# First unit of a sparse attention and its feed-forward layer: k and q loaded in turns, scores of each head pair as soon as it is there, masks as biases

## Chip, core and metric

The kernel runs on one core of a Trainium2 chip. The metric is the device time of one execution in microseconds (us), the median of several runs. PE is the tensor engine, DVE the vector engine, ACT the scalar engine, POOL is GpSimd and SP the sync engine.

## The reference

A block-sparse attention (4 batches, 8 heads, 768 positions, head size 64) is followed by a feed-forward layer with a quick GELU (3,072 tokens, width 512, inner width 2,048):

```python
k_sum = k.reshape(B, H, nb, 32, D).max(axis=3)      # 24 blocks of 32 positions
v_sum = v.reshape(B, H, nb, 32, D).mean(axis=3)
scores_l = where(abs(i - j) < 16, scale * q @ k.T, -1e9)
scores_s = scale * q @ k_sum.T + log(32)
a = softmax(concat([scores_l, scores_s]))
x = a @ concat([v, v_sum])                           # (tokens, 512)
h = x @ w_in
out = (h * sigmoid(1.702 * h)) @ w_out
```

Each query sees its neighbours within 15 positions and all 24 block rows. Inputs and output are float32 in HBM.

## The kernel before

The work is cut into eight *units* of 384 tokens, two for each batch. A unit has an attention part (scores, exponentials, values, normalization, transposition to `xT`) and a feed-forward part: `ff_in` makes 16 tiles `nt` of 128 inner columns (`ph`, then the GELU on ACT into `gT`), `ff_out` multiplies by `w_out` in 12 steps, called *slots*, of four matmuls (`po`). PE executes its instructions in the order in which the program writes them. The attention of a unit is laid between the feed-forward steps of the unit before it. The first unit has nothing to lie between: its attention is written out by hand, line by line, ahead of the loop over units. It covers batch 0, positions 0 to 383, and treats heads in four *pairs* `p`.

Every engine keeps the order of the program text (`keep_in_program_order`), so a line's place decides what stands behind it on its engine. An instruction that waits holds up all that follow on that engine.

The names for the first unit:

- `load_k(p)` loads one pair's keys in float32 as two DMAs, one from SP (first half of the positions) and one from ACT (second half); `load_q(p, 0)` loads the pair's first-half queries as one DMA, from SP for even and from ACT for odd pairs. The DMAs of these two queues share eight completion semaphores in turn, so that the ninth and later ones wait for an earlier landing before they are issued.
- `load_v0`, `load_w_in`, `load_w_out` and the second half of q (`load_q(p, 1)`) are issued from POOL. v and the weights are cast on the way.
- `cast_k`, `cast_q` make bfloat16 copies on the engine named; `k_turn`, `q_turn` transpose on PE; `k_own`, `q_copy` copy the result out of PSUM. `k_max` takes the block maxima.
- `s_turn(p)` makes the near scores of a pair in a PSUM tile of 1,024 columns (tag `big`, two buffers, shared with `k_turn`); `s_exp` is the exponential on ACT. `b_turn`, `b_exp` do the same for the block rows, `v_sum`, `v_copy` for the block sums of v; `av_near`, `av_blocks`, `v_norm` make the values; `x_turn` transposes them for the feed-forward part.
- Masks: `masks0` builds a tile on POOL by `affine_select`. Pairs 0 and 1 are multiplied by a tile of ones and zeros after the exponential (`s_mask`, on DVE); pairs 2 and 3 get a bias of -30000 from a matmul of that tile with the identity, ahead of the scores.
- `busy(n)` is n matmuls on zeros that nobody reads; `warmth(8)` the same, larger.

After the first unit, `plan0` says at which slot of the first unit's `ff_out` the second unit's attention is done: `q0` to `q3` transpose and copy the queries of the second half (`q_turn(i, 1)` and `q_copy(i, dve, 1)`, in the `big` buffers), `s0` to `s3` are scores, `v0`, `v1` values. The casts of these queries, `cast_q(dve, p, 1)`, stand after `ff_in` of `nt` 12 (pairs 0, 1) and 13 (pairs 2, 3). Slot -1 comes after the last `ff_in`:

```python
    plan0 = {-1: ["q0", "q1"], 0: ["q2", "q3"], 1: ["s0", "s1"], ...
```

For the third unit (batch 1), POOL loads k, v and q of that batch after w_out, and later writes the block-sum rows of v (`sum_dmas`, tile `vw` from `vs`).

Of the kernel before, what the change touches and what calls it, by code (L numbers as in the profile page):

```python
# [10 lines left out]
BF16 = mybir.dt.bfloat16  # L11
# [24 lines left out]
def kernel(  # L36
# [16 lines left out]
    NP = H // 2  # L53
# [51 lines left out]
    def load_v0(h0, h1):  # L105
        if h0 == 0:
            early["v"] = stage.tile([128, H, NJ, VC], BF16, name="vb", tag="vf")
            dve.memset(early["v"][..., D:VC], 1.0)
        pool.dma_start(out=early["v"][:, h0:h1, :, 0:D].rearrange("p h j d -> p (h j) d"),
                       in_=v[0, h0:h1].rearrange("h s d -> (h s) d")  # L110
                       .rearrange("(a p) d -> p a d", p=128))
# [68 lines left out]
    pool.affine_select(out=bm, in_=bm, compare_op=ALU.is_ge, fill=0.0, base=nb - 1,  # L180
                       pattern=[[block, 4]], channel_multiplier=-1)
    mk = consts.tile([128, NQ, QT], BF16, name="mk")
    mks = outp.tile([128, 2, 512], BF16, name="mk0", tag="osb")
    mk0, mk1 = mks[:, 0], mks[:, 1]
    dve.memset(mk0, 0.0)
    dve.memset(mk1, 1.0)
    BEFORE, AFTER, SIDE = HALF, HALF + 2 * window, 2 * window

    def masks0(mk0, fill):

        def out(ap, base, pattern, cp):
            pool.affine_select(out=ap, in_=ap, compare_op=ALU.is_ge, fill=fill,
                               base=base, pattern=pattern, channel_multiplier=cp)

        own = mk0[:, 0:HALF].rearrange("p (j c) -> p j c", c=128)
        out(own, window - 1, [[0, JH], [1, 128]], -1)
        out(own, window - 1, [[0, JH], [-1, 128]], 1)
        out(mk0[:, BEFORE:AFTER].rearrange("p (j c) -> p j c", c=window),
            -(128 - window + 1), [[0, JH - 1], [-1, window]], 1)
        out(mk0[:, AFTER:512].rearrange("p (j c) -> p j c", c=SIDE),  # L200
            -(SIDE - window + 1), [[0, JH], [1, SIDE]], -1)
# [83 lines left out]
    def cast_k(eng, p, half=None):  # L285
        if ("k", p) in cast:
            t = cast["k", p]
        else:
            if p == 0:
                kb2[0] = castp2.tile([128, NP, 2, JH, 2, D], BF16, name="kb", tag="kb")  # L290
            t = kb2[0][:, p]
        if half is None:
            copy(eng, t.rearrange("p e r h d -> p h (e r) d"),
                 raw["k", p].rearrange("p h e r d -> p h (e r) d"))
        else:
            copy(eng, t[:, half].rearrange("p r h d -> p h r d"), raw["k", p][:, half])
        cast["k", p] = t
# [38 lines left out]
    def busy(n):  # L336
        ps = pmm.tile([128, 512], F32, name="ps_w", tag="mm")
        for i in range(n):
            pe.matmul(out=ps[:, 0:128], lhsT=warm[:, 0:128], rhs=warm[:, 0:128],
                      start=True, stop=True)  # L340
# [66 lines left out]
    def k_turn(p):  # L407
        src = cast.pop(("k", p))
        big = st["K", p] = psb.tile([128, 1024], F32, name="ps_k", tag="big")
        for half in range(2):  # L410
            for r in range(JH):
                pe.matmul(out=at(big, half * 512 + r, [[JH, 128]]),
                          lhsT=src[:, half, r].rearrange("p h d -> p (h d)"),
                          rhs=ident, start=True, stop=True)
# [4 lines left out]
    def k_own(p, eng):  # L419

        copy(eng, own_keys(p).rearrange("p (e c) -> p e c", e=2),
             at(st["K", p], 0, [[512, 2], [1, HALF]]))

    def k_max(p):
        dve.tensor_reduce(out=ks0[p], in_=own_keys(p).rearrange("p (n c) -> p n c", c=block),
                          axis=AX.X, op=ALU.max)
# [25 lines left out]
    def s_turn(p):  # L452

        big = st["S", p] = psb.tile([128, 1024], F32, name="ps_s", tag="big")
        bias = p >= NP - 2
        if bias:
            for h in range(2):
                pe.matmul(out=big[:, h * 512:(h + 1) * 512], lhsT=ident, rhs=mk0, start=True,
                          stop=False, skip_group_check=True)

        def part(col, kj, q0, n):
            for h in range(2):
                r = slice(h * 64, h * 64 + 64)
                pe.matmul(out=big[:, h * 512 + col:h * 512 + col + n],
                          lhsT=own_keys(p)[r, kj * 128:(kj + 1) * 128],
                          rhs=qT[p][0][r, q0:q0 + n], start=not bias, stop=True,
                          skip_group_check=True)

        for j in range(JH):
            part(j * 128, j, j * 128, 128)  # L470
            part(AFTER + j * SIDE, j + 1, j * 128 + 128 - SIDE, SIDE)
            if j:
                part(BEFORE + (j - 1) * window, j - 1, j * 128, window)
# [9 lines left out]
    def s_exp(p):  # L483
        a = a_sb[p] = attp.tile([128, 2, 512], BF16, name="a_0", tag="a_sb")
        act.activation(out=a.rearrange("p h c -> p (h c)"), in_=st["S", p], func=ACT.Exp, scale=scale)

    def s_mask(p):
        dve.tensor_mul(a_sb[p], a_sb[p], mk1.unsqueeze(1).to_broadcast([128, 2, 512]))

    def b_turn(p):  # L490

# [113 lines left out]
    a_sb, x_sb, x2 = {}, {}, {}  # L605
# [330 lines left out]
    def exp_soon():  # L936
        act.activation(out=gate[:, 1:2], in_=gate[:, 0:1], func=ACT.Exp)


    dve.memset(gate, 0.0)  # L940
    for p in range(NP):
        load_k(p)
    exp_soon()
    for p in range(NP):
        load_q(p, 0)
    clear0(dve)
    dve.tensor_copy(out=identx, in_=ident)
    dve.memset(vs[:, :, D:VC], float(block))
    masks0(mk1, 0.0)
    warmth(8)  # L950

    cast_k(dve, 0, 0)
    cast_k(dve, 0, 1)
    k_turn(0)
    busy(3)
    cast_k(pool, 1, 0)
    cast_k("dve_alone", 1, 1)
    k_turn(1)
    busy(4)
    load_v0(0, 2)  # L960
    k_own(0, act)
    cast_k(act, 2, 0)
    cast_k(dve, 2, 1)
    load_v0(2, 4)
    load_v0(4, H)
    k_own(1, act)
    k_turn(2)
    busy(6)
    cast_k(dve, 3, 0)
    k_max(0)  # L970
    k_own(2, act)
    cast_k(act, 3, 1)
    cast_q(dve, 1, 0)
    cast_q(pool, 0, 0)
    k_turn(3)
    busy(4)
    cast_q(pool, 3, 0)
    k_own(3, act)
    q_turn(0)
    q_turn(1)  # L980
    k_max(1)
    cast_q(act, 2, 0)
    masks0(mk0, -30000.0)
    q_copy(0, dve)
    load_w_in(0, 512)
    busy(4)
    s_turn(0)
    q_copy(1, dve)
    q_turn(2)
    s_exp(0)  # L990
    q_turn(3)
    s_turn(1)
    k_max(2)
    q_copy(2, dve)
    load_w_in(512, 1024)
    b_turn(0)
    s_exp(1)
    q_copy(3, dve)
    b_turn(1)
    s_turn(2)  # L1000
    b_exp(0)
    v_sum(0)
    s_mask(0)
    s_turn(3)
    s_exp(2)
    load_w_in(1024, 1536)
    s_mask(1)
    v_copy(0)
    k_max(3)
    av_near(0)  # L1010
    s_exp(3)
    av_blocks(0, 0, D + 1)
# [43 lines left out]
    for p in range(NP):  # L1056
# [7 lines left out]
    plan1 = {0: ["t0"], 1: ["t1"], 2: ["s0", "s1"], 4: ["t2"], 5: ["t3"],  # L1064
             6: ["v0", "s2", "s3"], 8: ["x0"], 9: ["v1", "S0", "S1"], 11: ["x1", "S2", "S3"]}

    plan0 = {-1: ["q0", "q1"], 0: ["q2", "q3"], 1: ["s0", "s1"], 3: ["s2", "s3"], 6: ["v0", "v1"],
             9: ["x0"], 10: ["x1"]}

    w51 = vw[1].rearrange("p (j e) h c -> p j e h c", e=2)  # L1070
# [23 lines left out]
    for u in range(2):  # L1094
        todo = {}
        if u == 0:
            for p in range(NP):
                todo.setdefault(12 + p // 2, []).append(lambda p=p: cast_q(dve, p, 1))
        else:
            def value_rows():  # L1100
                vsum(1, range(NJ))
                block_sums()
                halo_dmas(w51, 0)
                sum_dmas(w51, 0)
                load_kc(2, range(6, H))
                load_vc(2)
                load_qc(2)

            todo = {0: [lambda: tk(0, 1)], 3: [lambda: tk(1, 1)], 5: [lambda: v_odd(1)],
                    9: [value_rows], 10: [lambda: tk(2, 1)], 13: [lambda: tk(3, 1)]}  # L1110
            ff_in(u, range(3))
        for nt in range(0 if u else N0, NT):
            if u == 0 or nt > 2:
                ff_in(u, (nt,))
            for f in todo.get(nt, ()):
                f()
        exp_soon()
        if u == 0:
            beside(1, -1)
            load_qc(1)  # L1120
            load_kc(2, range(6))
        order = [(ms, part) for ms in range(JH) for part in range(4)]
        if u == 0:

            order = [(ms, part) for part in range(4) for ms in range(JH)]
        for i, (ms, part) in enumerate(order):
            ff_out(u, ms, part)
            beside(u + 1, i)
            if u == 0 and i in (4, 7, 10):
                w_sums(i // 3 - 1)  # L1130
            if u == 1 and i == 2:
                w_sums(3)
            if u == 1 and i == 3:
                for g in range(2):
                    xk(g, 2)
# [122 lines left out]
```

## Time and profile before

| | us |
|---|---|
| median of four runs | 209.33 |
| lowest and highest | 208.01, 209.46 |
| profiled execution | 207.51 |
| its span, first to last instruction | 205.8 |
| PE busy | 198.3 |
| DVE busy | 146.9 |
| ACT busy | 124.6 |
| POOL busy | 92.7 |

The profile is of one execution; times in it are counted from the start of the span. Its rows name the engine, the operation and the tiles (out<-in). Nearly all instructions carry the line of the helper that keeps program order (L28), so one goes by the names of tiles: `kf`, `qf`, `vb` are the loaded k, q, v of batch 0; `kb`, `qb` their bfloat16 copies; `kx`, `qT` the transposed ones; `ps_...` PSUM tiles; `ph` and `po` the products of the feed-forward part. A busy PE is not PE at its peak, as ends of matmuls are modelled.

### The profile page before, as it was taken

What the parts mean: (1) busy time and instruction counts of PE and PEld (TensorE: products, weight loads), DVE (VectorE), ACT (ScalarE), POOL (GpSimd) and SP (SyncE); (2) the same over time, 40 slices, a digit from 0 to 9 for tenths busy, and PEclk for the clock granted to TensorE, in tenths of its full rate; (3) what the DMA queues carried; (4) which work ended last, traced back from release to release, by engine and by line L of the source; (5) the groups of instructions that cost most, each with busy time, mean ns of one, the idle gap of its engine ahead of it and who ended that gap; (6) DMA issues with size and microseconds to landing.
All of it is one profiled execution on the core that took longest, in us unless ns stands there. A gap on an engine that the chain in (4) does not pass through costs nothing.

```text
span 205.8 us, 5594 instructions
## 1 busy us (share of the span) xinstructions
PE 198.3 (96%) x2218; PEld 135.6 (66%) x2219; DVE 146.9 (71%) x423; ACT 124.6 (61%) x237; POOL 92.7 (45%) x165
## 2 busy tenths in 40 slices
PE   7799999999999999999999999999999999999993
PEld 2577655556655566566888866567888855568882
DVE  7698845798956769936757688589985856669331
ACT  2678677626675589677644657678627477881220
POOL 8968889399998953516998100301000000000000
PEclk9999999999999999999999999999999999999999
DMA  6999999999999999999999997993053250000323
GB/s 185 294 160 204 236 247 218 182 156 238 157 159 170 128 140 182 167 145 124 121 141 193 113 280 150 151 139 64 0 143 89 68 164 0 3 2 25 106 76 102
DMA packets 95010, 28.94 MB, mean 141 GB/s; under 512 B 82880, under 2 KB 92000, under 8 KB 94984
## 3 DMA queue, kind: packets, MB, share of 16 engines
q0 software_dynamic: 67920, 14.88, 84.2%
q1 hardware_dynamic: 25432, 12.53, 29.9%
q10 hardware_dynamic: 1632, 1.18, 1.9%
q8 instruction: 17, 0.28, 0.6%
q14 instruction: 9, 0.07, 0.1%
HBM read 27.26 MB, written 6.29 MB: 163 GB/s over the span
## 4 chain that ended last, share of the span: by engine, by line
PE 89%; DMA 4%; DVE 3%; ACT 1%; issue 0%; ACTq 0%; DVEq 0%
PE ph L28 31%; PE px L28 16%; PE po L28 10%; PE pw L28 8%; PE px_in L28 5%; PE ps_s L28 4%; PE py L28 4%; PE ps_av L28 4%; PE pw_in L28 4%; DMA kf<-in_k_dram 2%; DMA qf<-in_q_dram 2%; PE ps_t L28 1%; DVE qT L28 1%; PE ps_x L28 1%; PE ps_vs L28 1%; ACT L28 1%
## 5 line engine op out<-in xcount | busy, mean ns | idle before, releaser
L28 PE MATMUL ph<-xT,w_in_sb 128*128 128x384 f16 x384 | 65.1, 326 | 0.3 <-ACT xT L28 0.2
L28 PEld LDWEIGHTS <-w_in_sb 128*128 128x128 f16 x462 | 44.4, 98 | 29.2 <-issue 0.9
L28 ACT ACTIVATE gT<-ph 128x384 f16<-128x384 f32 x96 | 45.7, 491 | 19.1 <-PE ph L28 18.8
L28 PEld LDWEIGHTS <-gT 128*128 128x128 f16 x384 | 36.1, 98 | 11.9
L28 ACT ACTIVATE a_sb<-ps_s 128x768 bf16<-128x768 f32 x28 | 21.1, 806 | 8.4 <-PE ps_s L28 8.3
L28 PE MATMUL po<-w_out_sb,gT 128*128 128x512 f16 x96 | 23.4, 380 | 0.0
L28 PEld LDWEIGHTS <-ss 128*128 128x128 f16 x216 | 20.7, 98 | 2.6
L28 ACT ACTIVATE t<-px 128x256 f32<-128x256 f32 x21 | 8.1, 384 | 21.8 <-PE px L28 21.8
L28 DVE TENSOR_TENSOR a_sb<-a_sb,mk 128x768 bf16<-128x768 bf16 x28 | 15.2, 555 | 7.4 <-ACT a_sb L28 6.3
L28 PE MATMUL pw<-tb,gT 128*128 128x256 f16 x144 | 18.7, 273 | 0.0
L28 PE MATMUL px<-ta,ss 128*128 128x256 f16 x144 | 18.7, 273 | 0.0
L28 DVE TENSOR_TENSOR x<-ps_av,rc 128x384 f16<-128x384 f32 x28 | 15.6, 557 | 1.0
L28 POOL DMA_DIRECT2D vw<-in_v_dram x18 | 15.9, 932 | 0.0
L28 POOL DMA_DIRECT2D kb<-in_k_dram x16 | 13.2, 856 | 3.8 <-DMA w_out_sb<-in_moe_w_out_dram 3.4
L28 ACT ACT_TABLE_LOAD x10 | 12.8, 1283 | 3.1 <-issue 2.9
L28 POOL DMA_DIRECT2D vw<-vw x12 | 6.6, 564 | 17.5 <-DVE vw L28 16.0
L28 DVE TENSOR_TENSOR osb<-pw,t 128x256 f32<-128x256 f32 x18 | 7.5, 421 | 8.7 <-PE pw L28 5.3
L28 POOL DMA_DIRECT2D qb<-in_q_dram x16 | 13.4, 942 | 0.6 <-DMA vw<-in_v_dram 0.6
L28 DVE TENSOR_TENSOR ss<-gT 128x384 f16<-128x384 f16 (+4 forms) x18 | 7.5, 418 | 5.4 <-ACT gT L28 5.4
L28 DVE TENSOR_REDUCE ks<-kx 128x24 bf16<-128x768 bf16 x8 | 7.6, 946 | 3.8 <-DMA kx<-kb 3.8
L28 PEld LDWEIGHTS <-kx 64*128 64x128 bf16 x400 | 7.2, 95 | 4.6 <-issue 3.9
L28 PE MATMUL ps_s<-qT,kx 64*128 64x64 bf16 (+3 forms) x400 | 9.1, 190 | 0.5 <-DVE qT L28 0.3
(123 smaller groups left out, 312.1 us busy)
## 6 DMA issues: line engine op xcount, KB each, us to landing
out_dram<-osb SPq DMA_DIRECT2D x18, 256.0 KB, 4.5
vw<-in_v_dram POOLq DMA_DIRECT2D x18, 128.0 KB, 5.7
w_in_sb<-in_moe_w_in_dram POOLq DMA_DIRECT2D x4, 512.0 KB, 9.1
w_out_sb<-in_moe_w_out_dram POOLq DMA_DIRECT2D x4, 512.0 KB, 18.6
kb<-in_k_dram POOLq DMA_DIRECT2D x16, 96.0 KB, 5.0
qb<-in_q_dram POOLq DMA_DIRECT2D x16, 96.0 KB, 6.8
out_dram<-osb SPq DMA_DIRECT2D x12, 128.0 KB, 1.7
vw<-vs POOLq DMA_DIRECT2D x6, 148.5 KB, 4.4
```

The source lines that it names most:

```text
L28: r = f(*a, **kw)
```

## The change

k and q are loaded pair by pair: k0, q0, k1, q1, then the table load of the exponential, then k2, q2, k3, q3. Scores and exponentials of a pair are written as soon as its transposes are, instead of after all four pairs' keys. All four pairs get the bias matmul; the mask tile of ones and zeros, its memset and its affine selects, and `s_mask`, are gone. Casts change engines: POOL takes q0, the first half of k1, of k2, and q2; ACT takes q1 and q3; DVE all the rest. The three `load_v0` calls no longer follow one another on POOL: the casts of k2 and q2 stand between them, and the first `load_w_in` follows the third. Most `busy` calls are gone. Among the later work, the second unit's `q0` and `q1` move from slot -1 to after `ff_in` of `nt` 14 and 15, and `q2`, `q3` from slot 0 to slot -1.

```diff
     mk = consts.tile([128, NQ, QT], BF16, name="mk")
-    mks = outp.tile([128, 2, 512], BF16, name="mk0", tag="osb")
-    mk0, mk1 = mks[:, 0], mks[:, 1]
+    mk0 = outp.tile([128, 512], BF16, name="mk0", tag="osb")
     dve.memset(mk0, 0.0)
-    dve.memset(mk1, 1.0)
...
     def s_turn(p):
...
-        bias = p >= NP - 2
-        if bias:
-            for h in range(2):
-                pe.matmul(out=big[:, h * 512:(h + 1) * 512], lhsT=ident, rhs=mk0, start=True,
-                          stop=False, skip_group_check=True)
+        for h in range(2):
+            pe.matmul(out=big[:, h * 512:(h + 1) * 512], lhsT=ident, rhs=mk0, start=True,
+                      stop=False, skip_group_check=True)
...
-    def s_mask(p):
-        dve.tensor_mul(a_sb[p], a_sb[p], mk1.unsqueeze(1).to_broadcast([128, 2, 512]))
...
     dve.memset(gate, 0.0)
-    for p in range(NP):
+    load_k(0)
+    load_q(0, 0)
+    load_k(1)
+    load_q(1, 0)
+    exp_soon()
+    for p in (2, 3):
         load_k(p)
-    exp_soon()
-    for p in range(NP):
         load_q(p, 0)
     clear0(dve)
     dve.tensor_copy(out=identx, in_=ident)
     dve.memset(vs[:, :, D:VC], float(block))
-    masks0(mk1, 0.0)
+    masks0(mk0, -30000.0)
     warmth(8)
 
     cast_k(dve, 0, 0)
     cast_k(dve, 0, 1)
     k_turn(0)
+    cast_q(pool, 0, 0)
+    k_own(0, act)
     busy(3)
     cast_k(pool, 1, 0)
-    cast_k("dve_alone", 1, 1)
+    q_turn(0)
+    busy(3)
+    q_copy(0, dve)
+    cast_k(dve, 1, 1)
+    cast_q(act, 1, 0)
     k_turn(1)
-    busy(4)
+    s_turn(0)
     load_v0(0, 2)
-    k_own(0, act)
-    cast_k(act, 2, 0)
+    k_own(1, act)
+    k_max(0)
+    q_turn(1)
+    cast_k(pool, 2, 0)
+    s_exp(0)
     cast_k(dve, 2, 1)
+    q_copy(1, dve)
+    k_turn(2)
     load_v0(2, 4)
+    k_own(2, act)
+    s_turn(1)
+    k_max(1)
+    cast_q(pool, 2, 0)
+    s_exp(1)
+    cast_k(dve, 3, 0)
+    cast_k(dve, 3, 1)
     load_v0(4, H)
-    k_own(1, act)
-    k_turn(2)
-    busy(6)
-    cast_k(dve, 3, 0)
-    k_max(0)
-    k_own(2, act)
-    cast_k(act, 3, 1)
-    cast_q(dve, 1, 0)
-    cast_q(pool, 0, 0)
+    q_turn(2)
     k_turn(3)
-    busy(4)
-    cast_q(pool, 3, 0)
+    q_copy(2, dve)
+    cast_q(act, 3, 0)
     k_own(3, act)
-    q_turn(0)
-    q_turn(1)
-    k_max(1)
-    cast_q(act, 2, 0)
-    masks0(mk0, -30000.0)
-    q_copy(0, dve)
+    s_turn(2)
+    k_max(2)
+    b_turn(0)
+    b_turn(1)
+    s_exp(2)
+    q_turn(3)
+    q_copy(3, dve)
     load_w_in(0, 512)
-    busy(4)
-    s_turn(0)
...
+    b_exp(0)
+    s_turn(3)
+    k_max(3)
+    v_sum(0)
+    v_copy(0)
     load_w_in(512, 1024)
...
     load_w_in(1024, 1536)
...
     av_near(0)
     s_exp(3)
     av_blocks(0, 0, D + 1)
...
-    plan0 = {-1: ["q0", "q1"], 0: ["q2", "q3"], 1: ["s0", "s1"], 3: ["s2", "s3"], 6: ["v0", "v1"],
+    plan0 = {-3: ["q0"], -2: ["q1"], -1: ["q2", "q3"], 1: ["s0", "s1"], 3: ["s2", "s3"], 6: ["v0", "v1"],
              9: ["x0"], 10: ["x1"]}
...
         if u == 0:
             for p in range(NP):
                 todo.setdefault(12 + p // 2, []).append(lambda p=p: cast_q(dve, p, 1))
+            for nt in (14, 15):
+                todo.setdefault(nt, []).append(lambda nt=nt: beside(1, nt - 17))
```

More of the change, by code (lines that the diff above doesn't have):

```diff
@@ L465, in part @@
                           lhsT=own_keys(p)[r, kj * 128:(kj + 1) * 128],
-                          rhs=qT[p][0][r, q0:q0 + n], start=not bias, stop=True,
+                          rhs=qT[p][0][r, q0:q0 + n], start=False, stop=True,
                           skip_group_check=True)
@@ L954 @@
     k_turn(0)
+    cast_q(pool, 0, 0)
+    k_own(0, act)
     busy(3)
     cast_k(pool, 1, 0)
-    cast_k("dve_alone", 1, 1)
+    q_turn(0)
[3 more added lines that the diff above has]
+    cast_q(act, 1, 0)
     k_turn(1)
-    busy(4)
+    s_turn(0)
     load_v0(0, 2)
-    k_own(0, act)
-    cast_k(act, 2, 0)
+    k_own(1, act)
[3 more added lines that the diff above has]
+    s_exp(0)
     cast_k(dve, 2, 1)
+    q_copy(1, dve)
+    k_turn(2)
     load_v0(2, 4)
-    load_v0(4, H)
-    k_own(1, act)
-    k_turn(2)
-    busy(6)
-    cast_k(dve, 3, 0)
-    k_max(0)
-    k_own(2, act)
-    cast_k(act, 3, 1)
-    cast_q(dve, 1, 0)
-    cast_q(pool, 0, 0)
+    k_own(2, act)
[5 more added lines that the diff above has]
+    cast_k(dve, 3, 1)
+    load_v0(4, H)
+    q_turn(2)
     k_turn(3)
-    busy(4)
-    cast_q(pool, 3, 0)
+    q_copy(2, dve)
+    cast_q(act, 3, 0)
     k_own(3, act)
-    q_turn(0)
-    q_turn(1)
-    k_max(1)
-    cast_q(act, 2, 0)
-    masks0(mk0, -30000.0)
-    q_copy(0, dve)
-    load_w_in(0, 512)
-    busy(4)
-    s_turn(0)
[L988 to L994, printed above, removed]
-    load_w_in(512, 1024)
[L996 to L1005, printed above, removed]
+    s_turn(2)
[5 more added lines that the diff above has]
+    q_copy(3, dve)
+    load_w_in(0, 512)
+    b_exp(0)
[3 more added lines that the diff above has]
+    v_copy(0)
+    load_w_in(512, 1024)
     load_w_in(1024, 1536)
-    s_mask(1)
-    v_copy(0)
-    k_max(3)
     av_near(0)
```

## The prediction

> **What bounds the kernel now.** I read the page first, then the chain of waits from 20 to 36 us, the POOL and DVE timelines, and the DMA view in windows narrow enough to hold one issue each, so that its last column is that transfer's time from issue to landing.
>
> ```profile
> span 205.8 us, 5594 instructions
> DMA  6999999999999999999999997993053250000323
> PE 89%; DMA 4%; DVE 3%; ACT 1%; issue 0%; ACTq 0%; DVEq 0%
> ```
> The chain that ended last is PE for 89%: a microsecond of PE delay anywhere is a microsecond at the end, unless a wait further on swallows it. But the DMA engines are full from the start for two thirds of the span, so what is loaded early decides what is there later.
>
> ```profile
> 20.63 0.48 PE ph L28 x2
> ...
> 21.86 9.95 PE ph L28 x60
> 31.81 0.18 PE ps_q L28 x3
> 31.99 0.02 issue
> 32.02 1.45 DVE qT L28 x2
> 33.47 0.04 issue
> 33.51 0.33 PE ps_q L28 x3
> 33.84 0.86 PE po L28 x4
> ```
> (Start, length, what.) The first unit ends when `ph` starts at 20.63. PE then runs dense to 31.99, waits for two copies of q's second half (only one `po` slot covers them), and the second `po` slot comes about 33.67. From there the chain has no wait of note.
>
> ```profile
> 5.10 0.61 POOL L28 CAST kb<-kf 128x384 bf16<-128x384 f32 x1
> 5.66 3.63 POOL L28 DMA_DIRECT2D vb<-in_v_dram  x3
> 9.26 0.58 POOL L28 CAST qb<-qf 128x384 bf16<-128x384 f32 x1
> 11.92 0.51 POOL L28 CAST qb<-qf 128x384 bf16<-128x384 f32 x1 [2.08 <-DMA qf<-in_q_dram]
> 12.37 2.98 POOL L28 DMA_DIRECT2D w_in_sb<-in_moe_w_in_dram  x4
> 15.31 0.94 POOL L28 DMA_DIRECT2D qf<-in_q_dram  x1
> 16.20 0.80 POOL L28 DMA_DIRECT2D w_out_sb<-in_moe_w_out_dram  x1
> ```
> All v, w_in, second-half q and w_out go out from POOL, in this order, and the v loads go out back to back at 5.66, 6.83 and 7.86 (rows of 1.18, 1.05 and 1.44).
>
> ```profile
> w_in_sb<-in_moe_w_in_dram POOLq DMA_DIRECT2D x1, 512.0 KB, 6.4
> qf<-in_q_dram POOLq DMA_DIRECT2D x1, 768.0 KB, 13.4
> w_out_sb<-in_moe_w_out_dram POOLq DMA_DIRECT2D x1, 512.0 KB, 15.8
> vw<-vs POOLq DMA_DIRECT2D x1, 148.5 KB, 4.3
> ```
> Landings: w_in's first quarter 12.37+6.4=18.8, q's second half 28.7, w_out's first quarter 16.20+15.8=32.0, the sum rows 61.62+4.3=65.9. Against their users: `ph` at 20.63 (1.8 spare), DVE's casts of q (which wait for it), `po` at 32.04 (nothing spare), the values at 66.3 (0.4 spare). So POOL's stream of loads is a second bound, hidden just behind PE.
>
> ```profile
> 28.78 2.20 DVE L28 CAST qb<-qf 128x384 bf16<-128x384 f32 x4 [2.75 <-DMA qf<-in_q_dram]
> 32.02 2.72 DVE L28 CAST qT<-ps_q 128x384 bf16<-128x384 f32 x4 [1.03 <-PE ps_q L28]
> ```
> DVE waits 2.75 us for q's second half; its casts end at 30.98, and the copies then wait 1.03 for PE.
>
> **What the Trainium skill says.** "DMA: Bandwidth & Descriptors", section "Issuing engines are not separate DMA queues": all queues run on the same 16 engines. The trace agrees: the queues of SP and ACT move about 340 GB/s alone until 8 us, and what they move later is taken from POOL's. The same page, "SWDGE vs HWDGE vs iDMA": GpSimd computes the descriptors of its DMAs in software, and a load that casts has to go there; here POOL is busy about a microsecond per v load, and a v load cannot be issued while POOL waits for a cast's data. The same page, "Queues, rings and completion order": descriptors of a ring are consumed in order. Here w_in, q and w_out land in their order of issue, 2.6 us per quarter. "ScalarE: Activation LUTs", "What ACT_TABLE_LOAD costs": 1283 ns; the trace has 1283.
>
> **The change part by part.** *First unit.* Gone: two mask products on DVE (0.69 each), one memset (0.4), a second set of affine selects on POOL (1.5, 3.7 to 5.1), 15 filler matmuls (0.1 each and free of waits; the granted clock is 1.00 in every stretch, and I take it that it stays so). Added: four bias matmuls (0.39 each, pipelined 0.2), on a PE that has room then. Work is pulled forward. ACT issues its last loads until 6.84 as now (the last but one waits for the same landing, 5.92); then k copies 4x0.81, two q casts 0.52, exponentials 4x1.03, block exponential 0.49. With the waits of one on the other (each score needs the PSUM tile that the exponential before it frees, each k copy stands behind an exponential) I get the last two score groups at 12.6 and 14.5, v sums at 15.0, first values at 15.3 instead of 16.18, and `ph` possible at 19.6 to 19.9: 0.7 to 1.0 gained **there**, if data are.
>
> *POOL's queue: where the cost lies.* The built order puts on POOL: cast q0, cast k1, first v load, cast k2, second v load, cast q2, third v load, then w_in. SP's loads are now k0, q0, k1, k2, q2, and all have the same size as before, so the n-th on SP lands as the n-th did: second 5.04, third 1.83+5.2=7.0, fourth 2.34+6.0=8.3. Hence cast q0 5.1 to 5.7; k1 lands 7.05, cast to 7.7; first v load issued **7.7** (now 5.66); k2 cast to 9.5, second v load **9.5** (6.83); q2 cast to 11.1, third v load **11.1** (7.86), to 12.6; w_in at 12.6 (12.37). When do packets flow? An idle POOL queue showed its first packet 1.6 us after an issue with a row of 0.88 (issue at 94.85, packet at 96.4), 0.7 after the row's end. v is 6144 packets; at the 1,233 per us that the stretch 12 to 14 shows (2,467), the loads take 1.25, 1.25 and 2.5. First load 9.6 to 10.85, second 11.25 to 12.5, third 13.1 to 15.6. k and q on the other queues, 2.36 MB at 340 GB/s from 2.0, are through at 9.2 or so: the engines stand idle 0.4, 0.4 and 0.6 between. Now v is through at 14.5 (5,965 packets of POOL's queue from 8.3 to 14.5, the last few being w_in's). So everything behind v, in the same ring, is late by **1.1**; bounds 0.5 (packets flow before the row ends, k1 lands early) and 1.7 (DVE's casts slow POOL's rows).
>
> *What that does.* w_in lands at 19.9: `ph` starts about 20.0, still 0.6 earlier, chunks then come as fast as they are used. q's second half lands 29.9; the four casts end at 30.98+1.1=32.1. Moving q's transposes to after nt 14 and 15 puts all four before the first `po`; the third and fourth need the PSUM tiles that the first two copies free. DVE: 32.1, copies to 33.5 (1.45 from the chain), fourth transpose to 33.7, first `po` (0.86; w_out is there at 33.1) to 34.6. The second `po` starts at 34.6 to 34.7, against 33.67: **+1.0**. With a stream that is not late the same sum gives 33.56, a gain of 0.1: the casts, not PE, then set it. The moved slots cost nothing themselves; the wait that they cover has become DVE's casts.
>
> *Afterwards.* POOL waits for w_out's last quarter (40.2, then 41.3) before its eighth k load and then issues without pause to 62.2. The sum rows land at 67.0, their user comes at 67.3: no further wait. Nothing later gives back time on a PE chain. Sum: -0.9 in the first unit, covered by the late loads, and +1.0 net.
>
> **Base.** The sum stands against one execution: span 205.8, 207.51 with what lies around it. The median of the runs is 209.33, 1.8 above it; I add the same 1.0 to it: **210.3**.
>
> **Rivals.** (1) *The stream isn't late.* If the early packets of POOL's queue only took turns with k and q, whose traffic now ends before 9.3, and if the third v load's packets flow by 12.4, the engines have no idle stretch and nothing behind v moves. For it: full DMA engines throughout, so order alone would not matter. Against it: the three gaps in POOL's order above. It ends at -0.1; where the four casts are quick too (two of them took 0.4, one 1.14 beside POOL's memsets) at -0.4, and no further, as the sum rows have 0.4 to spare: 208.9 to 209.3, **not slower**. It decides from a delay under 0.1. (2) *PE gain carries through*: all 0.9 to 1.1 kept, 208.3. It needs q's second half 1 us earlier, and no queue shows a reason. (3) *DVE and POOL in each other's way*: a cast next to descriptor work took 1.15 instead of 0.45 (8.32); three such in a row, ahead of the third v load, make the stream 1.8 to 2.2 late, and the sum rows and values later: +1.8 to +2.3, 211.4.
>
> **Numbers.** About 0.5% (1.05 us) is what a measurement of this kernel can tell from no change. The forecast case has 0.62, its own range +0.5 to +1.6 (209.8 to 210.9), about as much above 1.05 as below. Rival 1 has 0.23, all within; rival 2 has 0.05; rival 3 has 0.10, slower. That makes faster 0.06, same 0.50, slower 0.44. Both signs have weight, so the range is 208.8 (rival 1) to 211.5 (rival 3).
>
> **What would show it.** Right: third v load issued near 11, first packets of POOL's queue near 9.6, gaps in it before 13; w_in landing near 19.9, q's second half near 29.9; DVE's casts ending near 32; second `po` near 34.6; first values about 15.3. Wrong: w_in landing by 19.0 and q's second half by 28.8 (rival 1), or PE waiting on something other than these loads before 35.

## The result, and the profile after

| | before | after |
|---|---|---|
| median, same chip, runs in turns | 208.54 (63 runs) | 209.37 (44 runs) |
| ratio after / before, 95% interval | | 1.0050 (1.0036 to 1.0064) |
| profiled execution | 207.51 | 210.08 |
| its span | 205.8 | 208.4 |

The change costs 1.04 us (0.0050 of 208.54). The ratio leaves out the two slow runs of the changed kernel, and it isn't the ratio of the two medians, which lie 0.83 apart. The two profiled executions lie 2.57 us apart, because that of before is a quick one of its kind (1.0 under its median) and that of after a slow one (0.7 over). So where sizes matter, a second execution of the unaltered changed kernel stands beside it (`e1_again`, 208.86 us).

The page of after, its lines for the span and for the chain that ended last:

```profile
span 208.4 us, 5560 instructions
PE 81%; DMA 11%; POOL 4%; DVE 2%; SPq 0%; issue 0%; DVEq 0%
```

PE has lost 8 points of the chain, and DMA (4% to 11%) and POOL have taken them. The chain itself, from its start to 37 us (start, length, what):

```profile
1.83 5.75 DMA kf<-in_k_dram
...
7.64 0.51 POOL kb L28
8.15 1.12 POOL vb L28
...
12.59 2.93 POOL w_in_sb L28 x4
15.52 16.32 DMA qf<-in_q_dram
...
31.86 2.03 DVE qb L28 x4
33.89 1.35 DVE qT L28 x2
...
35.28 0.33 PE ps_q L28 x3
35.61 1.51 PE po L28 x7
```

Read from the top: the first half of k1 lands at 7.58. POOL waits for it, casts it and only then issues the first v load; two more casts and two more v loads follow (in the timeline below), then w_in, then q's second half. That lands at 31.84, and DVE's casts and copies wait for it and PE for them. No score, exponential or `ph` is on it: the path runs through POOL's queue. In before this part of the chain was `ph` on PE. POOL's own timeline of after shows what stands between the loads:

```profile
7.64 0.51 POOL L28 CAST kb<-kf 128x384 bf16<-128x384 f32 x1 [1.66 <-DMA kf<-in_k_dram]
8.09 1.18 POOL L28 DMA_DIRECT2D vb<-in_v_dram  x1
9.27 0.52 POOL L28 CAST kb<-kf 128x384 bf16<-128x384 f32 x1
9.71 1.03 POOL L28 DMA_DIRECT2D vb<-in_v_dram  x1
10.74 0.52 POOL L28 CAST qb<-qf 128x384 bf16<-128x384 f32 x1
11.18 1.41 POOL L28 DMA_DIRECT2D vb<-in_v_dram  x1
```

The landings, in the DMA view of windows that hold one issue each (last column: issue to landing), after:

```profile
vb<-in_v_dram POOLq DMA_DIRECT2D x1, 384.0 KB, 8.2
w_in_sb<-in_moe_w_in_dram POOLq DMA_DIRECT2D x1, 512.0 KB, 9.4
qf<-in_q_dram POOLq DMA_DIRECT2D x1, 768.0 KB, 16.3
w_out_sb<-in_moe_w_out_dram POOLq DMA_DIRECT2D x1, 512.0 KB, 18.4
```

and in `e1_again`:

```profile
vb<-in_v_dram POOLq DMA_DIRECT2D x1, 384.0 KB, 5.9
w_in_sb<-in_moe_w_in_dram POOLq DMA_DIRECT2D x1, 512.0 KB, 7.6
qf<-in_q_dram POOLq DMA_DIRECT2D x1, 768.0 KB, 14.9
```

From the issues on POOL (12.58, 15.52 and 16.41 in after; 0.1 to 0.2 earlier in `e1_again`) w_in's first quarter lands at 22.0 and 20.1 (before 18.8), q's second half at 31.8 and 30.3 (28.8), w_out's first quarter at 34.8 and 33.5 (32.0). POOL issues w_in only 0.1 to 0.2 later than in before (12.37); what is late is v, 2.3 to 2.4 us at its first issue, and these loads come behind it in the same queue. DVE's casts and copies of after answer to it, with no wait left between the two rows:

```profile
31.86 2.03 DVE L28 CAST qb<-qf 128x384 bf16<-128x384 f32 x4 [3.21 <-DMA qf<-in_q_dram]
33.81 2.70 DVE L28 CAST qT<-ps_q 128x384 bf16<-128x384 f32 x4
```

The second `po` slot starts at 36.31 in after and 35.09 in `e1_again`, against 33.67: 2.64 and 1.42 later, and the profiled times are 2.57 and 1.35 longer. So in both executions the whole loss against before's one execution, to a tenth of a microsecond, is made before 37 us, and nothing after it gives any back.

The first unit did **not** become shorter. Its first values start at 16.52 and 16.37 (before 16.18), its first `ph` at 22.04 and 21.42 (before 20.63).

### The profile page after: what moved, and what is told of

The parts are those of the page before. It is cut to its first block, busy times and chain, and to the rows that moved or that the text cites. A ratio compares the mean times of both kernels' runs of the same rounds, so it can differ in the third digit from the quotient of the medians.

```text
span 208.4 us, 5560 instructions
## 1 busy us (share of the span) xinstructions
PE 197.8 (95%) x2206; PEld 135.4 (65%) x2208; DVE 145.5 (70%) x420; ACT 124.4 (60%) x236; POOL 91.9 (44%) x162
## 3 DMA queue, kind: packets, MB, share of 16 engines
q1 hardware_dynamic: 25432, 12.53, 30.3%
## 4 chain that ended last, share of the span: by engine, by line
PE 81%; DMA 11%; POOL 4%; DVE 2%; SPq 0%; issue 0%; DVEq 0%
PE ph L28 25%; PE px L28 15%; PE po L28 10%; DMA qf<-in_q_dram 8%; PE pw L28 8%; PE px_in L28 6%; PE py L28 4%; PE pw_in L28 4%; PE ps_av L28 3%; PE ps_s L28 3%; DMA kf<-in_k_dram 3%; POOL vb L28 2%; POOL w_in_sb L28 1%; PE ps_t L28 1%; DVE qb L28 1%; PE ps_x L28 1%
## 5 line engine op out<-in xcount | busy, mean ns | idle before, releaser
L28 ACT ACTIVATE gT<-ph 128x384 f16<-128x384 f32 x96 | 45.7, 490 | 19.3 <-PE ph L28 19.1
L28 POOL DMA_DIRECT2D kq<-in_q_dram x8 | 6.6, 842 | 7.7 <-DMA vw<-in_v_dram 7.7
```

Of the source, the lines that this page charges most:

```text
L28: r = f(*a, **kw)
```

## The experiments

Each ran in turns with the kernel before on the same chip. Times inside a span are of one profiled execution and scatter between executions; ratios are of many.

| kernel | ratio, 95% | first v load issued | first values | first `ph` | q's 2nd half lands | w_out lands | second `po` |
|---|---|---|---|---|---|---|---|
| before | 1 | 5.66 | 16.18 | 20.63 | 28.76 | 32.00 | 33.67 |
| after | 1.0050 (1.0036–1.0064) | 8.09 | 16.52 | 22.04 | 31.84 | 34.77 | 36.31 |
| e1_again | 1.0048 (1.0026–1.0070) | 7.92 | 16.37 | 21.42 | 30.34 | 33.51 | 35.09 |
| e2_v_together | 1.0067 (1.0046–1.0088) | 8.65 | 16.95 | 22.48 | 31.47 | 34.54 | 36.15 |
| e3_v_early | 1.0044 (1.0017–1.0072) | 5.87 | 16.54 | 21.12 | 28.29 | 31.49 | 34.79 |
| e4_old_slots | 1.0055 (1.0036–1.0074) | 7.47 | 15.92 | 21.45 | 30.69 | 33.59 | 34.85 |
| e5_late_stream | 1.0101 (1.0051–1.0151) | 5.67 | 15.93 | 20.45 | 31.65 | 34.40 | 35.65 |
| e6_new_slots | 0.9996 (0.9971–1.0020) | 5.83 | 16.23 | 21.11 | 29.44 | 32.43 | 34.78 |
| e7_mixed_slots | 0.9988 (0.9958–1.0018) | 5.86 | 16.61 | 21.63 | 29.82 | 32.85 | 34.44 |
| e8_pairs_v_first | 0.9990 (0.9968–1.0013) | | | | | | |
| e9_pairs_v_late | 1.0002 (0.9974–1.0030) | 5.53 | 15.54 | 20.38 | 29.34 | 32.59 | 33.84 |
| e10_pairs_v_first_2 | 0.9991 (0.9961–1.0021) | 5.54 | 15.89 | 20.63 | 28.29 | 31.47 | 33.45 |
| e11_bias_only | 1.0006 (0.9989–1.0023) | 5.58 | 17.60 | 22.05 | 29.54 | 32.59 | 35.21 |
| e12_w_in_late_small | 1.0048 (1.0032–1.0065) | 5.65 | 16.27 | 20.72 | 30.56 | 33.89 | 35.15 |

(e8_pairs_v_first is read by its ratio alone; e10 is the same kernel, with a trace. The profiled executions of e6 and e10 lost another 1.0 and 1.9 us after the second `po`, compared with before; in e10 a transfer for a later batch (`kx<-kb`) at 128.30 stands on the chain with 8.27 us. Their ratios, of many runs, show no loss.)

The row of before is a quick execution: e6, e7 and e11, whose ratios hold 1, have their second `po` at 34.4 to 35.2, where `e1_again` has 35.09. So one row can't tell 1 us. Taken together, q's second half landed at 29.4 on average in the four kernels with the early loads of before (before, e6, e7, e11) and at 31.0 in the three with those of the change (after, e1, e4), and the second `po` came at 34.5 and 35.4: about 1.6 and 0.9 later.

### The changed kernel again, and its slots taken back

`e1_again` is the changed kernel unaltered.

> The changed kernel unaltered, for the profile of another execution and as the partner of the three others. Stream theory (POOL's casts between the v loads leave gaps in the one queue that carries v, w_in, second-half q and w_out, so all of these land late, and DVE's casts of q then hold up PE): about 1.0 us slower than the kernel before; third v load issued near 11.2, gaps among v's packets, w_in's first quarter landing between 20 and 22, q's second half between 30 and 32, and the time following q's landing one for one. First-unit theory (the pair-by-pair order is itself slower on PE and ACT): same time, but ph would wait for xT on ACT or DVE, not for w_in. Slot theory (the moved q0 to q3 cost it): same time, and PE's wait near 33 to 35 would stand behind copies that start when PE has made its transposes, not when the casts end.

It repeats the ratio, with the same order on POOL and smaller delays; the third v load lands 5.9 instead of 8.2 after its issue. `e4_old_slots` takes back one part:

```diff
-    plan0 = {-3: ["q0"], -2: ["q1"], -1: ["q2", "q3"], 1: ...
+    plan0 = {-1: ["q0", "q1"], 0: ["q2", "q3"], 1: ...
-            for nt in (14, 15):
-                todo.setdefault(nt, []).append(lambda nt=nt: beside(1, nt - 17))
```

> The changed kernel with q0, q1 back in slot -1 and q2, q3 back in slot 0 of the first unit's second product. Stream theory: the loads stay late, so most of the loss stays: the first po, which waits for w_out, covers part of DVE's copies; 0.2 to 0.4 faster than the changed kernel, still 0.6 to 0.8 slower than before. Slot theory: back at the kernel before, 0.0. First-unit theory: no change, +1.0.

The loss stays: the moved slots aren't its cause, and the 0.2 to 0.4 that the old ones were expected to bring back can't be seen. Here the first `po` waits for w_out (landing 33.59, start 33.64).

### The slots alone, in the kernel before

`e6_new_slots` is the reverse of that diff, applied to before. `e7_mixed_slots` moves q0 and q1 as the change does and leaves q2 and q3 at slot 0.

> The kernel before with the new slots alone (q0 after nt 14, q1 after nt 15, q2 and q3 before the first po). Loads and first unit as before. By the prediction's sum: casts end at 31.0, DVE's copies 31.2 to 32.7, fourth transpose 32.8, second po near 33.7: -0.1 to +0.1. Slot theory: +0.7 to +1.0.

> The kernel before with q0 after nt 14, q1 after nt 15, but q2 and q3 still in slot 0, behind the first po: the first po then lies over DVE's copies, all four transposes wait for nothing. The first po still has to wait for w_out at 32.0: second po near 33.2, -0.3 to -0.45 against before. Slot theory (moved slots cost): +0.3 or more.

Both intervals hold 1: moving the slots neither costs nor brings what these runs can resolve.

### The masks alone

`e11_bias_only` makes all four masks by bias matmuls in the kernel before and takes out the mask products, the memset and the second set of affine selects:

```diff
-        bias = p >= NP - 2
+        bias = True
...
-    s_mask(0)
...
-    s_mask(1)
```

> The kernel before with one part of the change alone: all four pairs get their mask as a bias from a matmul, and the two mask products on DVE, the memset and the second set of affine selects are gone. If the masks cost nothing or bring nothing by themselves, as the prediction has it (DVE and PE have room there): ratio 0.999 to 1.001. If DVE's mask products stood on the path to the first values: 0.996 to 0.998, first values 0.4 or more earlier than 16.2. If the added matmuls stood on it: 1.001 to 1.003.

No difference that 22 runs can resolve (0.9989 to 1.0023). In its profiled execution k's loads landed late (first exponential at 13.74), which is why its row looks bad; the ratio doesn't show it.

### Is a late stream enough?

Both kernels are before with w_in, and all that POOL loads after it, held back behind an exponential; the first unit's computing isn't touched. `e5_late_stream` waits for the second exponential, `e12_w_in_late_small` for the first:

```diff
-    load_w_in(0, 512)
...
+    pool.tensor_copy(out=after, in_=a_sb[0][:, 0, 0:2])      # e5: a_sb[1]
+    load_w_in(0, 512)
+    load_w_in(512, 1024)
```

> The kernel before; only w_in's four loads, and with them all that POOL loads later, are issued after the second exponential (end about 14.94) instead of at 12.37, by a two-element copy on POOL that waits for it. The v loads and the first unit are left as they are. Stream theory: w_in starts to flow near 16.4 instead of 14.4, w_in lands at 20.8, q's second half at 30.8, w_out's first quarter at 34.0; the first po waits for it, the second po comes near 35.2: +1.4 to +1.7 against before. First-unit theory: w_in comes 0.2 late for ph, no more: 0.0 to +0.3.

> The kernel before with the first two w_in loads (and with them all later loads of POOL) issued behind the first exponential, by a copy of two elements on POOL that reads it: a smaller delay than in e5_late_stream. The first unit's computing is untouched. Expected: w_in issued about 13.9 instead of 12.37, landing 19.4 to 19.9, q's second half 29.4 to 30, ratio 1.002 to 1.005 if each microsecond of delay behind PE costs as in e5_late_stream; 0.999 to 1.001 if the first microsecond of delay is free.

Yes. The chain of `e12_w_in_late_small` shows the tiny copy, the issues and the transfer in the place that `ph` had:

```profile
13.93 0.18 POOL after L28
14.12 2.88 POOL w_in_sb L28 x4
16.99 13.57 DMA qf<-in_q_dram
...
30.59 1.86 DVE qb L28 x3
```

q's second half 1.8 late and w_out 1.9 late cost 0.48%, which is the loss of the changed kernel; 2.9 and 2.4 late cost 1.0%. The first `po` of `e5_late_stream` starts at 34.44, just after w_out at 34.40, and that of `e12_w_in_late_small` at 33.94, just after w_out at 33.89. (The profile puts that last wait down to a short row of ACT, which in before stands at the same place, 33.6, and holds up no `po`.) So a late stream is enough, though with the old slots w_out ends the wait, and in the changed kernel the copies of q.

### The stream mended, the first unit left

`e2_v_together` takes the casts of k2's first half and of q2 off POOL, so that the three v loads follow one another. `e3_v_early` takes k1's first half off it as well. All go to DVE, as a reduction that writes bfloat16 (the form called `dve_alone`):

```diff
-    cast_k(pool, 1, 0)            # e3 only
+    cast_k("dve_alone", 1, 0)
-    cast_k(pool, 2, 0)
+    cast_k("dve_alone", 2, 0)
-    cast_q(pool, 2, 0)
+    cast_q("dve_alone", 2, 0)
```

> The casts of k2 (first half) and q2 go from POOL to DVE, so that the three v loads follow one another on POOL behind k1's cast. Stream theory: v issued 8.1, 9.3, 10.3, w_in from 11.7; the gaps go, v is through near 15.0 (0.5 later than in the kernel before), q's second half lands near 29.3: 0.4 slower than before, 0.6 faster than the changed kernel. First-unit theory: no gain over the changed kernel, rather 0.3 slower, as DVE has two more casts. Slot theory: as the changed kernel, +1.0.

> As the run before, and k1's cast (first half) too goes from POOL to DVE: the v loads follow q0's cast at once. Stream theory: v issued from 6.0, w_in from 9.7, packets near 8.4 as in the kernel before; w_in lands by 18.9, q's second half by 28.8: -0.1 to +0.1 against before, 1.0 faster than the changed kernel, although DVE's copy of q0 now waits for k1. First-unit theory: slower than the changed kernel by 0.3 to 0.6. Slot theory: +1.0 against before.

`e2_v_together` brought nothing back: in its execution k1's first half landed at 8.15, the first v load went out at 8.65, and the stream was as late as in the changed kernel. So POOL's wait for k1 alone is enough to make the stream late. What the two casts between the loads add isn't separated, as k1 landed 0.6 later here than in after and DVE has two casts more.

`e3_v_early` mended the stream wholly (q at 28.29, w_out at 31.49, both earlier than in before), and **no gain shows**: 1.0044, with an interval from 1.0017 to 1.0072. Its chain says why:

```profile
7.31 0.55 DVE kb L28
...
9.51 1.06 DVE kb L28 x2
...
11.89 0.47 DVE qb L28
...
22.96 8.94 PE ph L28 x54
```

From k1's landing to 12.36 the chain is DVE without a pause, and `ph` runs dense from 22.96. In before the same matmul, the third of the 60 from 21.86, comes at about 22.2 (an estimate from 9.95 for 60), so the first unit is some 0.8 late. About 1.5 us of DVE's row are the casts that the edit moved there, so this run alone doesn't prove the same of the changed kernel. The trace of `e1_again` shows it, for one execution:

```profile
30.36 2.21 DVE L28 CAST qb<-qf 128x384 bf16<-128x384 f32 x4 [3.29 <-DMA qf<-in_q_dram]
32.03 0.33 PE L28 MATMUL ps_q<-ident,qb 128*128 128x128 bf16 x3
```

DVE's casts end at 32.57 and its copies follow at once. PE's first transpose for them, which follows the `ph` of `nt` 14, was done at 32.36. With q on time this execution would have gained some 0.2, no more (an estimate from these two rows). A second path ends nearly as late as the first: the first unit itself.

### Both mended

`e8_pairs_v_first` moves the three v loads up behind q0's cast, casts k1's first half on ACT and k3 in the reduction form, and sets q2 and q3 of the second unit back to slot 0:

```diff
     cast_q(pool, 0, 0)
+    load_v0(0, 2)
+    load_v0(2, 4)
+    load_v0(4, H)
     k_own(0, act)
     busy(3)
-    cast_k(pool, 1, 0)
+    cast_k(act, 1, 0)
...
-    cast_k(dve, 3, 0)
-    cast_k(dve, 3, 1)
+    cast_k("dve_alone", 3, 0)
+    cast_k("dve_alone", 3, 1)
```

> The changed kernel with all three v loads issued from POOL right behind q0's cast (the casts of k2 and q2 follow them on POOL, k1's first half is cast on ACT, k3's by the reduce form of copy on DVE), and with the slots of e7. Stream theory: loads as early as in the kernel before (q's second half by 28.8). If nothing but the stream and the slots held the changed kernel up, -0.3 to -0.5 against before. First-unit theory: first values at 16.3 or later, ph at 20.9 or later, DVE and ACT waiting on each other: +0.1 to +0.6.

> The kernel of e8_pairs_v_first once more, unaltered, for a second interval and a trace that can be read. Both causes mended: ratio to before 0.997 to 1.001, v loads issued at 5.7 to 7.9, w_in landing about 18.8, first values about 15.8, second po about 33.4. If that run was luck of its few executions: 1.003 or more.

Two runs, both at 0.999: the loss is gone, and no gain against before can be told. In the chain of `e10_pairs_v_first_2` neither POOL's stream nor a wait for q is left between 22 and 33 us:

```profile
22.47 8.94 PE ph L28 x54
31.40 0.17 PE ps_q L28 x3
31.57 0.65 PE ph L28 x4
32.22 0.17 PE ps_q L28 x3
32.39 0.86 PE po L28 x4
```

`e9_pairs_v_late` is the same without moving the v loads.

> The changed kernel with three of the edits of e8_pairs_v_first: k1's first half cast on ACT, [...]q2 and q3 of the second unit back at slot 0. The v loads stay where the change puts them, with the casts of k2 and q2 between. So the first unit's computing is mended and the stream is late. If the two bind side by side (what I now believe: the end of the first part is the later of the two): v loads issued about 7.5, 9.1 and 10.7, w_in landing 19.6 to 20.5, q's second half 29.7 to 30.6; ratio to before 1.002 to 1.005, since the stream alone still costs. If only the first unit's computing mattered: 0.998 to 1.000, as e8_pairs_v_first. If only the stream mattered: 1.005, as the changed kernel.

The expectation of the first load at 7.5 was a slip: with k1's cast gone from POOL, that load has only q0's cast ahead of it and went out at 5.53. The other two stayed behind their casts (8.09, 9.59), q and w_out came 0.6 late, and the time is that of before. So this run is no late stream with a mended first unit, as meant. It shows instead that moving **k1's first half** off POOL (with k3's other cast form and the slots) is enough, and that 0.6 of lateness in q and w_out is nearly covered: its first `po` waits for w_out and the second comes 0.17 later than in before. Which of the edits mended the first unit isn't separated: its DVE casts of k3 took 1.00 for two, in after 1.39 and in `e1_again` 0.89.

## Why the prediction was right, and where it was wrong

**The sign and the size** came out: +1.0 was forecast, +1.04 measured. The mechanism is the one that was named: the chains of after and `e1_again` run through it, and `e12_w_in_late_small` makes the same loss from a late stream alone. That 1.0 and 1.04 lie so close is in part luck, as the delay was set too small and the first unit's term had the wrong sign. The absolute forecast, 210.3, was 0.9 too high: its base of four runs lies 0.8 above the median of 63. So the measured 209.37 lies below the forecast's own range (209.8 to 210.9), though inside the whole one.

**POOL's queue: right.** v loads at 7.7, 9.5 and 11.1 were forecast; they went out at 8.09, 9.71 and 11.18, and in `e1_again` at 7.92, 9.55 and 11.07. The first three packets of POOL's queue came between 9.6 and 10.0 (forecast 9.6), and in windows of half a microsecond its stream shows two dips, 343 packets from 11.5 to 12 and 290 from 13 to 13.5, where a full window has about 600.

**The delay behind v: right in kind, undersized.** 1.1 was forecast, bounds 0.5 and 1.7. w_in, q and w_out were late by 3.2, 3.1 and 2.8 in after and by 1.3, 1.6 and 1.5 in `e1_again`. k1's first half landed 0.3 to 0.5 later than the forecast 7.05, and the third v load seems to have kept some packets until long after the rest. It landed at 19.39, and from 18 to 19.3 us the DMA view of after has:

```profile
DMA packets 284, 0.25 MB, mean 196 GB/s; under 512 B 38, under 2 KB 284, under 8 KB 284
```

In before the small packets fall to 38 between 15 and 16 us and to none in the next, but up to 14 per us pass later too, so only part of the 38 can be v's. It isn't the rate of the queue: from 16 to 22 us the DMA engines moved 1.19 MB in after and 1.22 in `e1_again`, though w_in landed 1.9 apart. A third load that lands at 16.9 or later is seen in `after`, `e1_again`, `e2_v_together` and `e4_old_slots`, whose third v load is issued at 10.6 or later, and in no other execution read here. Why a load's last packets should stay behind wasn't tried.

**The first unit: the step that failed.** Forecast were 0.7 to 1.0 gained, with first values at 15.3 and `ph` possible at 19.6 to 19.9. The changed kernel lost 0.2 to 0.3 at the first values and 0.8 to 1.4 at `ph`. The loss at the first values is made in two places. The exponentials of before:

```profile
12.76 2.17 ACT L28 ACTIVATE a<-ps_s 128x1024 bf16<-128x1024 f32 x2 [0.69 <-PE ps_s L28]
15.20 2.14 ACT L28 ACTIVATE a<-ps_s 128x1024 bf16<-128x1024 f32 x2
```

and the first three of after:

```profile
9.91 1.02 ACT L28 ACTIVATE a<-ps_s 128x1024 bf16<-128x1024 f32 x1
12.03 1.02 ACT L28 ACTIVATE a<-ps_s 128x1024 bf16<-128x1024 f32 x1 [0.25 <-PE ps_s L28]
14.55 1.02 ACT L28 ACTIVATE a<-ps_s 128x1024 bf16<-128x1024 f32 x1
```

The first starts 2.9 earlier, but in before four follow each other 1.1 to 1.3 apart. In the changed kernel a k copy on ACT or a wait for a score stands ahead of each, and they are 1.8 to 2.5 apart. Against `e9_pairs_v_late`, 0.57 of after's 0.98 at the first values is made before the first exponential (9.91 against 9.34), which stands on ACT behind the copy of k1, and 0.4 by one stretched cast. The sum took casts on DVE at the time they take alone. Beside POOL's casts and descriptor work one took three times that, as this row of `e1_again` shows:

```profile
9.32 1.44 DVE L28 CAST kb<-kf 128x384 bf16<-128x384 f32 x1 [0.71 <-DMA kf<-in_k_dram]
```

against the same cast in `e9_pairs_v_late`:

```profile
8.82 0.47 DVE L28 CAST kb<-kf 128x384 bf16<-128x384 f32 x1 [0.66 <-DMA kf<-in_k_dram]
```

The Trainium skill, "SBUF — State Buffer", section "SBUF: two separate sides", has GpSimd and certain VectorE instructions (in a two-port mode, or with two SBUF inputs) share one pair of ports as an exclusive lock, where whichever starts first makes the other wait for the whole instruction. Whether this is it stays open. Beside the 1.44, POOL's cast ran from 9.10 to 9.62 and its v load's row to 10.59; a cast that waits and then takes 0.47 would have waited until about 10.3 (an estimate), which is the end of neither. The 0.47 ran beside a v load's row that lasted until 9.12, and no run here takes the lock apart. Rival 3 had this effect, but on POOL's rows, which kept their 1.0 to 1.4; it was DVE that lost. The stretched cast costs about 0.4: where a long one stands in a pair's path, the exponentials are 2.5 apart (12.03 to 14.55 in after, 9.74 to 12.21 in `e1_again`), otherwise 2.1 or 2.2.

From the first values to `ph`, after loses to the late stream, 0.86 for the third v load and 0.27 for w_in, and `e1_again` to a wait for which the profile names no releaser:

```profile
19.44 0.36 PE L28 MATMUL ps_vt<-vb,E 128*32 128x64 bf16 x24 [0.86 <-DMA vb<-in_v_dram]
19.88 0.33 PE L28 MATMUL ps_av<-vb,a 128*16 128x65 bf16 x9 [0.73 <-issue]
```

(The first row is of after, the second of `e1_again`.) Such a wait stands in this stretch in e2, e3, e4, e9 and e10 as well (0.26 to 1.15), and at another instruction in e6 and e7 (0.66 and 0.79), so it isn't the pair order that brings it; before, e5, e11 and e12 have none, and in after PE waits for v there. In all eight it ended 2.2 to 2.5 us after a packet of the queue that the DMA view calls `q8 instruction`. That PE waited for its own instructions is the likely reading, and no run tests it. It matters for the forecast: the kernel with the quickest first unit, e9, has first values at 15.54, 0.64 earlier than before, but then this wait of 0.53, and its `ph` at 20.38 is only 0.25 earlier. Without the wait PE would have been ready at about 19.9, and as ACT's first copy of `xT` ended at 20.0, `ph` would have come near 20.1 (an estimate): most of the gain, still short of the forecast 19.6 to 19.9.

**The cover: half of it was missing from the text.** "-0.9 in the first unit, covered by the late loads" had one bound behind the other. There were two side by side, each worth about 1 us in the executions read: the stream (`e12_w_in_late_small`) and the first unit's own computing (`e3_v_early`, and the two rows of `e1_again`). Mending one only showed the other. The forecast total survived a wrong first-unit term by luck: the stream was the later of the two, by 0.2 in `e1_again`.

**Slots and masks at no cost: right** (`e4`, `e6`, `e7`, `e11`). **Afterwards, right:** sum rows landing at 67.0 were forecast; the two landings are 67.1 and 67.7, before their user (68.92), and the shift at the second `po` is the shift of the whole time.

**Rivals.** (1) the stream isn't late: fell with the landings. (2) a first-unit gain that carries through: fell with the first values, and even mended no gain was measured. (3) see above. What stays open: the typical delay of the stream, since the two executions of the changed kernel gave 1.3 to 3.2 and the averages above 1.6, from few traces; and the wait of PE that has no releaser.

## What to carry to other kernels

Look for instructions that wait for data ahead of a DMA issue on the same engine: here a 0.5 us cast, whose data came at 7.6, put off the first v load by 2.4 us, the landings of all that follows in that queue came 1.3 to 3.2 later, and it showed 25 us on. When a change hurts two paths that run side by side, mending one brings nothing back, and its ratio reads like a refutation; only mending both tells (1.0044 and then 0.999). Compare the shift at a late checkpoint with the shift of the whole execution before sizing anything from a pair of profiles, since one execution of each kernel can differ by 2.6 us where many runs differ by 1.0; and read several executions before calling one term right or wrong.

## What the runs showed of the hardware that was not expected

- Loads landed late though the DMA engines moved as much: the third v load of after landed at 19.39, 3.6 later than in before, and w_in 1.9 later than in `e1_again`, with 1.19 and 1.22 MB moved from 16 to 22 us. That the landing hangs on a few packets left behind is a reading, not shown.
- PE waited 0.26 to 1.15 us in eight executions with no releaser that the profile shows, each time until 2.2 to 2.5 us after a packet of the queue `q8 instruction` (in `e1_again` 17.6 and 19.88).
- The same DVE cast of 128x384 from float32 took 0.35 to 1.44 us, the longest beside a cast and a load's row of POOL; POOL's own casts took 0.50 to 0.61 in the rows shown of both kernels.
- The third load of SP's queue, the same size and issued at about 1.83 in each kernel, landed between 6.8 (`e10_pairs_v_first_2`) and 8.15 (`e2_v_together`) over the executions read; where POOL's loads stood behind the cast of that data, the first v load went out between 7.47 (`e4_old_slots`) and 8.65 (`e2_v_together`).
